# Attention and feed-forward on one core: eight chunks of three tiles in place of nine chunks of two and three

## The chip, the core and the metric

The kernel runs on one core of one Trainium2 chip. The metric is the device time of an execution in microseconds (us). Engines in the text: PE is TensorE, ACT is ScalarE, DVE is VectorE, POOL is GpSimd, SP is SyncE, which here issues nearly all DMAs.

## The reference

Attention over 4 sequences with 8 heads, 768 positions and head size 64. Each position sees a window of the last 128 positions and the first 4 positions (the sinks). The heads' outputs are put side by side (3072 tokens of 512) and go through a feed-forward with d_ff = 2048 and an ELU between two products.

```python
scores = scale * np.matmul(q, k.transpose(0, 1, 3, 2))
rel = pos[:, None] - pos[None, :]
keep = (pos[None, :] < n_sink) | ((rel >= 0) & (rel < window))
scores = np.where(keep, scores, -1e9); scores -= scores.max(-1, keepdims=True)
a = np.exp(scores); a = a / (a.sum(-1, keepdims=True) + 1e-9)
x = heads_side_by_side(np.matmul(a, v))          # 3072 x 512, fp32
h = x @ w_in                                     # 3072 x 2048
g = np.where(h > 0, h, np.exp(np.minimum(h, 0)) - 1)
return (g @ w_out).astype(np.float32)
```

The weights come as float64, 16 MB in all. Results must have about fp32 accuracy, so nearly every product is made of fp16 halves: a value is split into a high half and a residue, and hi*hi, lo*hi and hi*lo are added up in PSUM.

## The kernel before

**Tiles and chunks.** A tile is 128 tokens; there are 24, six a sequence, and tile g is number t = g % 6 in its sequence. Nine chunks (`CHUNKS`) of two or three tiles are worked off in turn: three of two tiles, then six of three. For a chunk, `attention(c)` makes x (four head pairs of 128 columns, `xs[c, q]`) and `feed_forward(c, f0, f1, start)` runs the products over 16 slices f of d_ff: a first stage of 12 matmuls into `h` (L845), the ELU on ACT (L854), POOL or DVE (L856) and DVE (L857), the split of g on ACT (L859) and POOL (L866), and a second stage of 3 matmuls of 512 columns a tile into `acc` (L873). The second stage of an f follows two f later (`LAG`).

**Attention.** Each chunk has one step for each tile and head pair: scores on PE into the banks s0 and s1 (L662 and L663 for split fp16 keys, L668 for fp32), mask and maximum on DVE (L683), exponential on ACT (L688), one plus reciprocal (L692, L697). Keys come by DMA into two slots `kqs` (L568), the first two pairs of chunk 0 ahead of all else (L1249). In the first `DUP` chunks scores are plain fp32 products; in later ones ACT and DVE split the keys first (L577 to L579). A tile with t = 0 has one key block of 128 columns, others have two (260 columns with the sinks). Chunk 0 (`c < PLAIN`) goes on in fp32: a diagonal of the reciprocals on POOL (L704), a product with it on PE that turns the probabilities (L710), an eviction on ACT or DVE (L714), the values in fp32 (L727). All other chunks split the probabilities (L742, L743), turn them with a DMA (L761), and visit PE once for all tiles of a head pair (L775), from chunk `PAIRS` = 3 on once for two pairs. L817 and L818 then make x.

**Weights.** 32 pieces (piece 2f for the first stage, 2f+1 for the second) come by DMA (L354, 512 KB each, at most five ahead of the piece that has been split), and each is rebuilt and split by ACT (L347), DVE (L348), ACT (L507) and POOL (L508, twice).

**Parts.** `PARTS` lets the first two chunks take turns: f 0 to 6 of chunk 0, 0 to 12 of chunk 1, then the rest of chunk 0 and of chunk 1. A chunk's first part stores its sums in `out` through the buffers `sv`; after its second part these are loaded again and added (L912 on).

**Order.** All of this is a list of tasks with rough costs. `Plan.order` puts PE's tasks at wanted positions, works due times backward, runs a list schedule forward, and then applies the changes of `SHIFTS` (each a seed of a random shift of due times or of a line of PE's tasks) one upon the other. Engines then issue in that order; SP issues a load when its task comes up. `with_idle_products` fills planned holes of PE in the first 100 us with products on a constant (L446). Reductions that check the range of inputs (`seen`, `check_v`, `check_kq`) are DVE tasks in the later chunks.

Of the kernel before, what the change touches and what calls it, by code (L numbers as in the profile page):

```python
# [10 lines left out]
F32 = mybir.dt.float32  # L11
# [10 lines left out]
P = 128  # L22
# [20 lines left out]

CHUNKS = [[0, 6], [12, 18], [1, 7], [13, 14, 15], [16, 17, 19], [20, 21, 22], [23, 2, 3], [4, 5, 8], [9, 10, 11]]
SIZES = tuple(len(c) for c in CHUNKS)

HALF = NF // 2
PARTS = [(0,0,7),(1,0,13),(0,7,16),(1,13,16)] + [(c, 0, NF) for c in range(2, len(SIZES))]
LAG = 2
ROUNDS = 8  # L50
SHIFTS = [600047, 600054, 600066, 600067, 600150, 600157, 600163, 600185, 600194, 600295, 600400, 600467, 600483, 600849, 601310, 601684, 602239, 602260, 603167, 603862]
VISIT = 2
# [3 lines left out]
KEEP = 1  # L56
DUP = 3
AHEAD = 5
# [8 lines left out]
PE_T, PE_V = 0.25, 0.13  # L67
RINGS = dict(tp=2, tp_=2, kqs=2, kq=3, vs=2, vm=2, vt=7, sk=2, e=3, st=6, pq=3, pt=6, g=2, gh=3, x=8, wv=4, s0=1, s1=1, po=1, h=2, wu=2, sv=2, wps=1, raw=6)

# [333 lines left out]
def fast_path(tc, ctx, first, kq, vx, wt, out, low, spread, copied, numbers, flag):  # L403
# [26 lines left out]
    xb = pool.tile([P, RINGS["x"] * 2 * TOK_MAX], F16, name="x")  # L430
    sv = rows("sv", [P, DM], F32)
    wv = rows("wv", [P, 512], F32)
# [114 lines left out]
    def attention(c):  # L547
# [12 lines left out]
        def split_keys(h):  # L560
# [13 lines left out]
            if (c, h) not in first["kq"]:  # L574
                ld = add("SP", 0.4, lambda: nc.sync.dma_start(raw, kq[:, o : o + kw]), lat=dma_us(P * kw * 4))
                ld.spare = LATE
            th = add("ACT", act_us(kw), lambda: nc.scalar.activation(hi, raw, AF.Copy, scale=Q_SCALE), deps=[ld])  # L577
# [7 lines left out]
        def vraw(g):  # L585

            if g not in raw_of or raw_of[g][3] < c - KEEP:
                fresh = g not in raw_of
                st, users = vs[slot("vs")], []
                ld = None  # L590
                if not fresh or g not in first["vs_"]:
                    ld = add("SP", 0.4, lambda: nc.sync.dma_start(st, vx[:, g * VT : (g + 1) * VT]), lat=dma_us(P * VT * 4))
                    ld.spare = LATE if c >= DUP else 0.0
                ring("vs", [ld] if ld else [], users)
                raw_of[g] = st, ld, users, c
            raw_of[g] = *raw_of[g][:3], c
            return raw_of[g][:3]
# [15 lines left out]
        def sink_rows(b):  # L613

            if b not in sk_of:
                st, sk, users = vs[slot("vs")], sks[slot("sk")], []
                o = SINKS + b * VT
                ld = add("SP", 0.4, lambda: nc.sync.dma_start(st, vx[:, o : o + VT]), lat=dma_us(P * VT * 4))
                ld.spare = LATE if c >= DUP else 0.0
                va = add("ACT", act_us(VT), lambda: nc.scalar.activation(sk, st, AF.Copy, scale=V_SCALE), deps=[ld])  # L620
                vb = add("DVE", 0.13 + 0.00108 * VT, lambda: nc.vector.scalar_tensor_tensor(sk[64:96, :], st[64:96, :], V_SCALE, sk[64:96, :], ALU.mult, ALU.subtract), deps=[va])
                ring("vs", [ld], [va, vb])
                ring("sk", [va], users)
                sk_of[b] = sk, vb, users
# [200 lines left out]
    def feed_forward(c, f0, f1, start):  # L825
# [77 lines left out]
        for i in range(nt):  # L903
            rows_ = out[CHUNKS[c][i] * P : (CHUNKS[c][i] + 1) * P, :]
            if f1 < NF:
                o = sv[slot("sv")]
            else:
                o = wv[slot("wv")]
            ld = None
            if f0 > 0:  # L910
                ld = add("SP", 0.4, lambda o=o, rows_=rows_: nc.sync.dma_start(o, rows_), deps=[saved[c, i]], lat=dma_us(P * DM * 4))
                ev = add("DVE", dve_us(DM), lambda o=o, i=i: nc.vector.scalar_tensor_tensor(o, acc[i], 1.0 / (G_SCALE * W_SCALE), o, ALU.mult, ALU.add), deps=[s2[i], ld])  # L912
            elif i % 2 or f1 < NF:
                ev = add("ACT", act_us(DM), lambda o=o, i=i: nc.scalar.activation(o, acc[i], AF.Copy, scale=1.0 / (G_SCALE * W_SCALE)), deps=[s2[i]])
            else:
                ev = add("DVE", dve_us(DM), lambda o=o, i=i: nc.vector.tensor_scalar(o, acc[i], 1.0 / (G_SCALE * W_SCALE), None, ALU.mult), deps=[s2[i]])
            sto = add("SP", 0.4, lambda o=o, rows_=rows_: nc.sync.dma_start(rows_, o), deps=[ev], lat=dma_us(P * DM * 4))
            ring("sv" if f1 < NF else "wv", [ld or ev], [sto])
            saved[c, i] = sto
            evacs[i] = ev  # L920

    saved, exps_done, last_g = {}, [], [None]
    start = 0
# [6 lines left out]

    seen = [add("DVE", 0.5, lambda k=k: nc.vector.tensor_reduce(w_top[:, k : k + 1], w[k][:, 0, :], AX.X, ALU.max, apply_absolute_value=True), deps=[w_done[k][0], exps_done[NF * 4 + 2 * k]]) for k in range(NW)]
    def check_v(c, after):
# [26 lines left out]
    for c in range(len(SIZES)):  # L959
        check_v(c, exps_done[NF * 4 + 3 * c])  # L960
    for i in range((len(SIZES) - DUP) * NP):
        check_kq(DUP + i // NP, i % NP, len(SIZES) * NP + i, exps_done[NF * 6 - 4 + 2 * i])

# [33 lines left out]

HINTS = dict(PE=8, ACT=127, DVE=120, SP=61)
E = mybir.EngineType
# [285 lines left out]
```

## Time and profile before

| | us |
|---|---|
| median of 3 runs | 611.33 (611.16 to 611.52) |
| the profiled execution | 611.1 |
| its span, first to last instruction | 609.3 |
| PE busy | 601.2 |
| DVE, ACT, POOL busy | 481.8, 428.1, 308.3 |
| DMA: moved, share of the span | 105.21 MB, 67.4% on SP's queue |

A busy PE is not a PE at useful work: the products on a constant count as busy. Timelines list a run of like instructions as one row with start, length and count; the start of the next row tells when PE went on, since matmuls overlap at their ends.

### The profile page before, as it was taken

How to read it: one execution, taken by the hardware profiler on the slowest of the kernel's cores; microseconds unless marked ns; L12 is line 12 of the kernel's file. 1: busy time of each engine (PE TensorE's matmuls, PEld its weight loads, DVE VectorE, ACT ScalarE, POOL GpSimd, SP SyncE). 2: the span in 40 equal slices, each digit the busy share in tenths (PEclk: the TensorE clock that was granted, in tenths of full speed). 3: DMA queues.
4: the chain of work that ended last, by engine and by line, in shares of the span. 5: the costliest groups of instructions: out<-in, count | busy, mean ns of one | idle time of the engine just before them, and what ended most of it. 6: DMA issues, size and time to landing. Idle time of an engine off the chain costs nothing.

```text
span 609.3 us, 13575 instructions
## 1 busy us (share of the span) xinstructions
PE 601.2 (99%) x4590; PEld 365.7 (60%) x4590; DVE 481.8 (79%) x1211; ACT 428.1 (70%) x1202; POOL 308.3 (51%) x587
## 2 busy tenths in 40 slices
PE   9899999999999999999999999999999999999997
PEld 6666666667765655656565555655656565556664
DVE  6989989799998468899799888799988977543333
ACT  7999999789888567876767766677766756422222
POOL 5876999546555344354544554355554534222221
PEclk9999999999999999999999999999999999999999
DMA  8999987689787346696678955599784883524201
GB/s 311 330 233 267 318 262 227 152 221 209 147 183 188 79 100 118 164 269 126 173 161 247 228 144 133 132 251 221 149 182 105 225 161 75 111 73 113 62 1 56
DMA packets 125998, 105.21 MB, mean 173 GB/s; under 512 B 100580, under 2 KB 100836, under 8 KB 125924
## 3 DMA queue, kind: packets, MB, share of 16 engines
q1 hardware_dynamic: 125780, 104.17, 67.4%
q8 instruction: 37, 0.61, 0.4%
q14 instruction: 37, 0.30, 0.2%
q10 hardware_dynamic: 144, 0.13, 0.1%
HBM read 72.82 MB, written 7.34 MB: 132 GB/s over the span
## 4 chain that ended last, share of the span: by engine, by line
PE 94%; DVE 2%; ACT 2%; issue 1%; POOL 0%; POOLq 0%; DVEq 0%
PE h L845 41%; PE acc L873 40%; PE po L775 3%; PE s L662 3%; PE s L663 3%; PE s L775 2%; PE s L668 1%; PE po L873 1%; PE acc L446 1%; ACT e L688 1%; ACT wu L347 0%; DVE e L683 0%; DVE wv L348 0%; ACT w L507 0%; PE s L780 0%
## 5 line engine op out<-in xcount | busy, mean ns | idle before, releaser
L845 PE MATMUL h<-x,w 128*128 128x384 f16 (+1 forms) x1728 | 273.6, 308 | 0.2
L845 PEld LDWEIGHTS <-w 128*128 128x128 f16 x1728 | 168.4, 98 | 84.4 <-issue 0.7
L866 POOL TENSOR_TENSOR gl<-g,gh 128x384 f16<-128x384 f32 (+1 forms) x144 | 129.3, 898 | 140.7 <-ACT gh L859 132.3
L873 PE MATMUL acc<-w,gh 128*128 128x512 f16 (+1 forms) x768 | 190.3, 375 | 0.0
L873 PEld LDWEIGHTS <-gh 128*128 128x128 f16 x800 | 76.9, 98 | 65.4 <-ACT g L854 1.0
L854 ACT ACTIVATE g<-h 128x384 f32<-128x384 f32 (+1 forms) x144 | 65.0, 451 | 66.8 <-PE h L845 64.9
L743 DVE SCALAR_TENSOR_TENSOR pq<-e,st,pq 128x256 f16<-128x256 f32 (+1 forms) x176 | 100.1, 589 | 14.5 <-ACT pq L742 13.7
L688 ACT ACTIVATE e<-e,st 128x260 f32<-128x260 f32 (+1 forms) x192 | 93.3, 487 | 24.1 <-DVE st L683 23.1
L873 PE MATMUL acc<-w,gl 128*128 128x512 f16 (+1 forms) x384 | 107.8, 375 | 0.0
L859 ACT ACTIVATE gh<-g 128x384 f16<-128x384 f32 (+1 forms) x144 | 69.6, 484 | 54.1 <-DVE g L857 53.4
L683 DVE CUSTOM_DVE_ANT_0 e<-s,m 128x260 f32<-128x260 f32 (+1 forms) x192 | 75.5, 399 | 20.8 <-PE s L663 18.0
L742 ACT ACTIVATE pq<-e,st 128x256 f16<-128x256 f32 (+1 forms) x176 | 79.7, 490 | 13.2 <-DVE st L697 11.9
L857 DVE SCALAR_TENSOR_TENSOR g<-g,h 128x384 f32<-128x384 f32 (+1 forms) x144 | 72.4, 503 | 12.3 <-POOL g L856 11.1
L856 POOL TENSOR_SCALAR g<-g 128x384 f32<-128x384 f32 (+1 forms) x77 | 42.0, 545 | 63.5 <-ACT g L854 62.7
L856 DVE TENSOR_SCALAR g<-g 128x384 f32<-128x384 f32 (+1 forms) x67 | 27.9, 417 | 50.2 <-ACT g L854 49.5
L873 PEld LDWEIGHTS <-gl 128*128 128x128 f16 x400 | 39.1, 98 | 44.2 <-POOL gl L866 0.7
L577 ACT ACTIVATE kq<-kqs 128x912 f16<-128x912 f32 (+1 forms) x48 | 48.5, 1010 | 8.7 <-PE s L663 6.1
L508 POOL TENSOR_TENSOR w<-wv,w 128x256 f16<-128x256 f32 x64 | 53.0, 846 | 2.8 <-ACT w L507 2.1
L692 POOL TENSOR_SCALAR st<-st 128x2 f32<-128x2 f32 x83 | 25.0, 301 | 47.0 <-ACT e L688 41.9
L578 DVE SCALAR_TENSOR_TENSOR kq<-kqs,kq 128x528 f16<-128x528 f32 (+1 forms) x48 | 39.3, 820 | 2.6 <-ACT kq L577 2.1
L662 PE MATMUL s<-kq 128*128 128x260 f16 x144 | 39.5, 275 | 0.0
L663 PE MATMUL s<-kq 128*128 128x260 f16 x144 | 39.5, 274 | 0.0
(105 smaller groups left out, 671.1 us busy)
## 6 DMA issues: line engine op xcount, KB each, us to landing
raw<-in_wt_dram SPq DMA_DIRECT2D x32, 512.0 KB, 5.8
kqs<-in_kq_dram SPq DMA_DIRECT2D x24, 522.0 KB, 3.9
kqs<-in_kq_dram SPq DMA_DIRECT2D x24, 456.0 KB, 4.2
vs<-in_vx_dram SPq DMA_DIRECT2D x34, 256.0 KB, 3.5
vm<-in_kq_dram SPq DMA_DIRECT2D x24, 261.0 KB, 4.2
out_dram<-wv SPq DMA_DIRECT2D x23, 256.0 KB, 2.4
vm<-in_kq_dram SPq DMA_DIRECT2D x24, 228.0 KB, 4.3
vm<-in_vx_dram SPq DMA_DIRECT2D x9, 512.0 KB, 5.3
```

The source lines that it names most:

```text
L662: nc.tensor.matmul(sp[:, :wd], q, hi[:, c0 : c0 + wd], start=True, stop=False)
L683: red = add("DVE", 0.08 + 0.00103 * wd, lambda ee=ee, me=me, sp=sps[e], m=m, wd=wd, to_score=to_score: nc.vector.tensor_tensor_reduce(ee, ...
L688: ex = add("ACT", 0.278 + 0.00083 * wd, lambda ee=ee, me=me, rs=rs[:, e : e + 1]: nc.scalar.activation(ee, ee, AF.Exp, bias=me, scale=-1.0 ...
L742: a = add("ACT", act_us(nb * P, True), lambda src=src, hi=hi, re=re: nc.scalar.activation(hi, src, AF.Copy, scale=re), deps=[rr])
L743: b = add("DVE", 0.45 if nb == 2 else 0.3, lambda src=src, hi=hi, lo=lo, re=re: nc.vector.scalar_tensor_tensor(lo, src, re, hi, ALU.mult, ...
L845: nc.tensor.matmul(hp[:, :n], win[:, part, d, :], xx[:, :n], start=k == 0, stop=k == 3 * ND - 1)
L854: a = add("ACT", 0.13 + 0.00091 * n, lambda gf=gf, hp=hp, sums=sums: nc.scalar.activation(gf, hp[:, :n], AF.Exp, scale=1.0 / G_SCALE, accu ...
L856: b = add("DVE", 0.06 + 0.00057 * n, lambda gf=gf: nc.vector.tensor_scalar(gf, gf, -1.0, G_SCALE, ALU.add, ALU.mult), deps=[a], slow=2.1, ...
L857: b = last_g[0] = add("DVE", dve_us(n), lambda gf=gf, hp=hp: nc.vector.scalar_tensor_tensor(gf, gf, 0.0, hp[:, :n], ALU.min, ALU.max), dep ...
L859: th = add("ACT", act_us(n), lambda gf=gf, gh=gh: nc.scalar.activation(gh[:, :n], gf, AF.Copy), deps=[b])
L866: tls.append(add("POOL", pool_us(cut), lambda gl=gl, gf=gf, gh=gh, cut=cut: nc.gpsimd.tensor_tensor(gl[:, :cut], gf[:, :cut], gh[:, :cut], ...
L873: nc.tensor.matmul(bank[:, cs], gg[:, i * P : (i + 1) * P], wout[:, part, cs], start=f == f0 and k == 0, stop=f == f1 - 1 and k == 2)
```

## The change

The tiles are grouped anew: eight chunks of three. `PARTS` runs each chunk in one piece, and what stored, loaded and added partial sums goes, with the buffers `sv`; the room gives `vs` a third slot. `DUP` falls to 2, so the first two chunks (six tiles, as before) have fp32 scores. `PLAIN` stays 1, so chunk 0 with its fp32 path has three tiles. `LATE`, a margin on loads in the plan, applies from chunk 3 as before. The range checks hang on other exponentials of the same kind. `SHIFTS` is another list, of 36 seeds in place of 20 (left out below), and `HINTS`, which places a branch hint in each engine's queue, has new counts.

```diff
--- before.py
+++ after.py
@@ -41,20 +41,19 @@
 V_MAX, EXP_MAX, W_MAX, W_MIN = 31.0, 2900.0, 65000.0, 0.25
 
 
-CHUNKS = [[0, 6], [12, 18], [1, 7], [13, 14, 15], [16, 17, 19], [20, 21, 22], [23, 2, 3], [4, 5, 8], [9, 10, 11]]
+CHUNKS = [[0, 6, 12], [18, 19, 20], [21, 22, 23], [13, 14, 15], [16, 17, 1], [2, 3, 4], [5, 7, 8], [9, 10, 11]]
 SIZES = tuple(len(c) for c in CHUNKS)
 
-HALF = NF // 2
-PARTS = [(0,0,7),(1,0,13),(0,7,16),(1,13,16)] + [(c, 0, NF) for c in range(2, len(SIZES))]
+PARTS = [(c, 0, NF) for c in range(len(SIZES))]
 LAG = 2
 ROUNDS = 8
...
 VISIT = 2
 PAIRS = 3
 LATE = 1.0
 SPARE = 0.1
 KEEP = 1
-DUP = 3
+DUP = 2
 AHEAD = 5
 HELD = 3
 HALVES = (slice(0, DM // 2), slice(DM // 2, DM))
@@ -65,7 +64,7 @@
 V_AT0 = 5.0
 T_AT = 3.5
 PE_T, PE_V = 0.25, 0.13
-RINGS = dict(tp=2, tp_=2, kqs=2, kq=3, vs=2, vm=2, vt=7, sk=2, e=3, st=6, pq=3, pt=6, g=2, gh=3, x=8, wv=4, s0=1, s1=1, po=1, h=2, wu=2, sv=2, wps=1, raw=6)
+RINGS = dict(tp=2, tp_=2, kqs=2, kq=3, vs=3, vm=2, vt=7, sk=2, e=3, st=6, pq=3, pt=6, g=2, gh=3, x=8, wv=4, s0=1, s1=1, po=1, h=2, wu=2, wps=1, raw=6)
 
 
 def key_tiles(ch):
@@ -428,7 +427,6 @@
     ghs = rows("gh", [P, TOK_MAX], F16)
     gls = rows("gl", [P, TOK_MAX], F16, RINGS["gh"])
     xb = pool.tile([P, RINGS["x"] * 2 * TOK_MAX], F16, name="x")
-    sv = rows("sv", [P, DM], F32)
     wv = rows("wv", [P, 512], F32)
     wu = rows("wu", [P, 512], I32)
     rawb = pool.tile([P, RINGS["raw"], 1025], I32, name="raw")
@@ -573,7 +571,7 @@
             ld = None
             if (c, h) not in first["kq"]:
                 ld = add("SP", 0.4, lambda: nc.sync.dma_start(raw, kq[:, o : o + kw]), lat=dma_us(P * kw * 4))
-                ld.spare = LATE
+                ld.spare = LATE if c >= 3 else 0.0
             th = add("ACT", act_us(kw), lambda: nc.scalar.activation(hi, raw, AF.Copy, scale=Q_SCALE), deps=[ld])
             tk = add("DVE", 0.155 + 0.00106 * kc, lambda: nc.vector.scalar_tensor_tensor(lo, raw[:, :kc], Q_SCALE, hi[:, :kc], ALU.mult, ALU.subtract), deps=[th], slow=1.5)
             tq = add("DVE", 0.18 + 0.00106 * qc, lambda: nc.vector.scalar_tensor_tensor(hi[D:, kc:], raw[D:, kc:], Q_SCALE, hi[D:, kc:], ALU.mult, ALU.subtract), deps=[th], slow=1.5)
@@ -590,7 +588,7 @@
                 ld = None
                 if not fresh or g not in first["vs_"]:
                     ld = add("SP", 0.4, lambda: nc.sync.dma_start(st, vx[:, g * VT : (g + 1) * VT]), lat=dma_us(P * VT * 4))
-                    ld.spare = LATE if c >= DUP else 0.0
+                    ld.spare = LATE if c >= 3 else 0.0
                 ring("vs", [ld] if ld else [], users)
                 raw_of[g] = st, ld, users, c
             raw_of[g] = *raw_of[g][:3], c
@@ -616,7 +614,7 @@
                 st, sk, users = vs[slot("vs")], sks[slot("sk")], []
                 o = SINKS + b * VT
                 ld = add("SP", 0.4, lambda: nc.sync.dma_start(st, vx[:, o : o + VT]), lat=dma_us(P * VT * 4))
-                ld.spare = LATE if c >= DUP else 0.0
+                ld.spare = LATE if c >= 3 else 0.0
                 va = add("ACT", act_us(VT), lambda: nc.scalar.activation(sk, st, AF.Copy, scale=V_SCALE), deps=[ld])
                 vb = add("DVE", 0.13 + 0.00108 * VT, lambda: nc.vector.scalar_tensor_tensor(sk[64:96, :], st[64:96, :], V_SCALE, sk[64:96, :], ALU.mult, ALU.subtract), deps=[va])
                 ring("vs", [ld], [va, vb])
@@ -902,24 +900,16 @@
             nt -= 1
         for i in range(nt):
             rows_ = out[CHUNKS[c][i] * P : (CHUNKS[c][i] + 1) * P, :]
-            if f1 < NF:
-                o = sv[slot("sv")]
-            else:
-                o = wv[slot("wv")]
-            ld = None
-            if f0 > 0:
-                ld = add("SP", 0.4, lambda o=o, rows_=rows_: nc.sync.dma_start(o, rows_), deps=[saved[c, i]], lat=dma_us(P * DM * 4))
-                ev = add("DVE", dve_us(DM), lambda o=o, i=i: nc.vector.scalar_tensor_tensor(o, acc[i], 1.0 / (G_SCALE * W_SCALE), o, ALU.mult, ALU.add), deps=[s2[i], ld])
-            elif i % 2 or f1 < NF:
+            o = wv[slot("wv")]
+            if i % 2:
                 ev = add("ACT", act_us(DM), lambda o=o, i=i: nc.scalar.activation(o, acc[i], AF.Copy, scale=1.0 / (G_SCALE * W_SCALE)), deps=[s2[i]])
             else:
                 ev = add("DVE", dve_us(DM), lambda o=o, i=i: nc.vector.tensor_scalar(o, acc[i], 1.0 / (G_SCALE * W_SCALE), None, ALU.mult), deps=[s2[i]])
             sto = add("SP", 0.4, lambda o=o, rows_=rows_: nc.sync.dma_start(rows_, o), deps=[ev], lat=dma_us(P * DM * 4))
-            ring("sv" if f1 < NF else "wv", [ld or ev], [sto])
-            saved[c, i] = sto
+            ring("wv", [ev], [sto])
             evacs[i] = ev
 
-    saved, exps_done, last_g = {}, [], [None]
+    exps_done, last_g = [], [None]
     start = 0
     for c, f0, f1 in PARTS:
         if f0 == 0:
@@ -928,7 +918,7 @@
         start += 2 * (f1 - f0)
 
 
-    seen = [add("DVE", 0.5, lambda k=k: nc.vector.tensor_reduce(w_top[:, k : k + 1], w[k][:, 0, :], AX.X, ALU.max, apply_absolute_value=True), deps=[w_done[k][0], exps_done[NF * 4 + 2 * k]]) for k in range(NW)]
+    seen = [add("DVE", 0.5, lambda k=k: nc.vector.tensor_reduce(w_top[:, k : k + 1], w[k][:, 0, :], AX.X, ALU.max, apply_absolute_value=True), deps=[w_done[k][0], exps_done[NF * 3 + 2 * k]]) for k in range(NW)]
     def check_v(c, after):
         t, n = vm[slot("vm")].rearrange("p a w -> p (a w)"), SIZES[c] * P
         src = vx[:, (ENDS[c] - SIZES[c]) * VT : ENDS[c] * VT].rearrange("p (g w) -> p g w", g=SIZES[c])
@@ -957,9 +947,9 @@
         seen.extend(new)
 
     for c in range(len(SIZES)):
-        check_v(c, exps_done[NF * 4 + 3 * c])
+        check_v(c, exps_done[NF * 3 + 3 * c])
     for i in range((len(SIZES) - DUP) * NP):
-        check_kq(DUP + i // NP, i % NP, len(SIZES) * NP + i, exps_done[NF * 6 - 4 + 2 * i])
+        check_kq(DUP + i // NP, i % NP, len(SIZES) * NP + i, exps_done[len(exps_done) - 6 - 2 * ((len(SIZES) - DUP) * NP - i)])
 
     def before():
         for r, most in ((es_of[:, 1:], EXP_MAX), (v_top, V_MAX)):
@@ -995,7 +985,7 @@
 VERBOSE = False
 
 
-HINTS = dict(PE=8, ACT=127, DVE=120, SP=61)
+HINTS = dict(PE=8, ACT=94, DVE=120, SP=45)
 E = mybir.EngineType
 QUEUES = dict(PE=E.PE, ACT=E.Activation, DVE=E.DVE, SP=E.SP)
```

## Rows read from the trace of the kernel before

**Rows 1.** The page: the span, and each engine's busy time, share and instructions.

```profile
span 609.3 us, 13575 instructions
...
PE 601.2 (99%) x4590; PEld 365.7 (60%) x4590; DVE 481.8 (79%) x1211; ACT 428.1 (70%) x1202; POOL 308.3 (51%) x587
```

**Rows 2.** Windows: length, busy us of PE, PEld, DVE, ACT, POOL; clock, DMA.

```profile
10.00:20.00 10.00, 8.75 (x68) 6.07 (x67) 8.76 (x27) 9.82 (x31) 8.81 (x13) 1.00 0.96 354
20.00:30.00 10.00, 9.00 (x78) 6.43 (x78) 8.48 (x35) 9.41 (x33) 7.97 (x12) 1.00 0.94 347
27.72:61.90 34.18, 33.63 (x273) 21.71 (x270) 30.83 (x97) 34.18 (x117) 24.87 (x44) 1.00 0.96 260
62.00:110.00 48.00, 48.00 (x381) 31.46 (x382) 44.55 (x88) 46.92 (x131) 45.64 (x57) 1.00 0.81 258
178.00:250.00 72.00, 72.00 (x543) 41.63 (x542) 52.42 (x133) 51.31 (x136) 30.58 (x61) 1.00 0.54 121
400.00:500.00 100.00, 100.00 (x778) 58.09 (x777) 90.03 (x204) 69.88 (x188) 50.78 (x107) 1.00 0.83 182
```

**Rows 3.** PE's timeline, the start: start, us, line, operation, count.

```profile
4.27 0.49 PE L668 MATMUL s<-kqs 64*128 64x128 f32 x4
...
8.33 0.49 PE L668 MATMUL s<-kqs 64*128 64x128 f32 x4
...
9.40 0.44 PE L727 MATMUL po<-pt,vs 128*64 128x128 f32 x4
...
13.89 0.49 PE L668 MATMUL s<-kqs 64*128 64x128 f32 x4
...
19.13 0.70 PE L668 MATMUL s<-kqs 64*128 64x128 f32 x4 [0.58 <-DVE st L683]
...
27.72 1.47 PE L845 MATMUL h<-x,w 128*128 128x256 f16 x12
```

**Rows 4.** SP's timeline: the load of the third head pair's keys.

```profile
6.31 0.33 SPq L568 DMA_DIRECT2D kqs<-in_kq_dram  x1
```

**Rows 5.** The view of tile kqs, 6 to 8 us: that load's landing.

```profile
DMA to landing us min/median/max: 6.8/6.8/6.8
```

**Rows 6.** Windows, PE alone: the DMA's GB/s is the last column.

```profile
8.00:10.00 2.00, 2.00 (x18) 1.00 1.02 416
12.00:14.00 2.00, 1.83 (x17) 1.00 1.04 408
```

**Rows 7.** PE's timeline: first stages of successive f, two tiles, then three.

```profile
72.52 1.47 PE L845 MATMUL h<-x,w 128*128 128x256 f16 x12
...
75.12 1.47 PE L845 MATMUL h<-x,w 128*128 128x256 f16 x12
...
538.35 2.11 PE L845 MATMUL h<-x,w 128*128 128x384 f16 x12
...
542.24 2.11 PE L845 MATMUL h<-x,w 128*128 128x384 f16 x12
```

**Rows 8.** PE's timeline: two visits, an f with a wide score.

```profile
38.54 0.25 PE L775 MATMUL po<-pt,vh 128*64 128x128 f16 x2
...
39.00 1.48 PE L845 MATMUL h<-x,w 128*128 128x256 f16 x12
...
60.45 1.47 PE L845 MATMUL h<-x,w 128*128 128x256 f16 x12
...
63.80 1.47 PE L845 MATMUL h<-x,w 128*128 128x256 f16 x12
...
67.81 0.30 PE L775 MATMUL po<-pt,vh 128*64 128x128 f16 x4
...
68.61 1.04 PE L873 MATMUL acc<-w,gh 128*128 128x512 f16 x4
```

**Rows 9.** Groups of POOL by shape: count, busy us, mean ns, idle before.

```profile
L866 POOL TENSOR_TENSOR gl<-g,gh 128x384 f16<-128x384 f32 x95 | 90.4, 952 | 126.0 <-ACT gh L859 121.0 <-issue 4.2
...
L508 POOL TENSOR_TENSOR w<-wv,w 128x256 f16<-128x256 f32 x64 | 53.0, 846 | 2.8 <-ACT w L507 2.1
```

More of the change, by code (lines that the diff above doesn't have):

```diff
@@ L41 @@
 V_MAX, EXP_MAX, W_MAX, W_MIN = 31.0, 2900.0, 65000.0, 0.25
-CHUNKS = [[0, 6], [12, 18], [1, 7], [13, 14, 15], [16, 17, 19], [20, 21, 22], [23, 2, 3], [4, 5, 8], [9, 10, 11]]
+CHUNKS = [[0, 6, 12], [18, 19, 20], [21, 22, 23], [13, 14, 15], [16, 17, 1], [2, 3, 4], [5, 7, 8], [9, 10, 11]]
 SIZES = tuple(len(c) for c in CHUNKS)
-HALF = NF // 2
-PARTS = [(0,0,7),(1,0,13),(0,7,16),(1,13,16)] + [(c, 0, NF) for c in range(2, len(SIZES))]
+PARTS = [(c, 0, NF) for c in range(len(SIZES))]
 LAG = 2
 ROUNDS = 8
-SHIFTS = [600047, 600054, 600066, 600067, 600150, 600157, 600163, 600185, 600194, 600295, 600400, 600467, 600483, 600849, 601310, 601684, 602239, 602260, 603167, 603862]
+SHIFTS = [7000020, 7000061, 7000067, 7000128, 7000202, 7000237, 7000246, 7000268, 7000272, 7000307, 7000441, 7000520, 7000523, 7000539, 7000579, 7000614, 7000907, 7001079, 7001093, 7001174, 7001179, 7001758, 7001996, 7002607, 7002617, 7002623, 7002624, 7002735, 7002873, 7003005, 7003193, 7004872, 7005450, 7009092, 7012293, 7016138]
 VISIT = 2
```

## The prediction

> **What bounds the kernel now.** I read the page first: TensorE (PE) counts as busy for 601.2 of 609.3 us [rows 1], so only what PE has to do, and the places where it can't do it, can move the time. The table by stages comes second [rows 2]: from 62 us on PE is busy for the whole of every stretch, while ACT, DVE and POOL have room (in 178 to 250, ACT 51.3 and POOL 30.6 of 72 us; DVE comes near its limit only in 400 to 500, 90.0 of 100, and PE still never waits). Before that it is the other way round: from 10 to 62 us ACT is busy nearly without a break (34.18 of 34.18 in 27.72 to 61.90), DVE and POOL follow, and 62 to 110 has POOL at 45.64 of 48. That is where the 32 weight pieces are split, beside the attention of the first chunks. The third view, PE's timeline of the first 28 us [rows 3], shows what the busy share hides: between the scores and values stand filler products on a constant (L446), which are no work. The first product of the feed-forward is at 27.72.
>
> So the end is: the start T of the feed-forward, plus the work PE still has to do then, plus the holes after T. I forecast each.
>
> **The work after T.** The feed-forward is the same 24 tiles in other groups. One f (a slice of 128 of d_ff) takes 2.60 us with two tiles and 3.89 with three [rows 7]. 48 f of two tiles become 32 of three: 48 x 2.60 = 124.8 becomes 32 x 3.89 = 124.5, so -0.3. The wider matmul gains nothing here. Splitting the first two chunks in parts, and its removal, changes no matmul either: what goes are four stores, four loads and adds of partial sums, on SP and on ACT and DVE after 27 us; PE reads none of it, so they count as nothing, hidden by PE's own work; without that cover they are four evictions of about half a us.
>
> The set of tiles with fp32 scores keeps its size (0, 6, 12, 18, 1, 7 become 0, 6, 12, 18, 19, 20: four first tiles of a sequence, two others), so the scores cost the same in both. What differs is tile 12: it moves from chunk 1 into chunk 0, the plain one, where probabilities are turned on PE and values are fp32. Its four scores move ahead of T (0.49 us by the row, 0.42 up to the next start [rows 3], so -1.7 after T). Its fp16 values vanish. Two visits show their price: 38.54 to 39.00 for two tiles of one key block, 67.81 to 68.61 for two tiles of two blocks [rows 8], so 0.34/2 = 0.17 a block and 0.12 a visit. That is 4 x 0.17 = 0.7 less, and with 18 visits in place of 20 another 0.2. The sum of work after T: -0.3 - 1.7 - 0.7 - 0.2 = **-2.9 us**. The checks keep their number and their distance from the end of the kernel; they run on DVE, where PE never waited for them.
>
> Break-even is therefore at T = 27.72 + 2.9 = 30.6, if the holes after T stay the same.
>
> **The start T.** Chunk 0 now has 12 steps (three tiles, four head pairs) in place of 8, and its plain path is on the way to T. Before, four steps came at once, one each (8.33 - 4.27)/3 = 1.35 us; then came a wait until 13.89 for the keys of the third head pair; then four more at (19.13 - 13.89)/3 = 1.75; and 8.6 us after the last score the feed-forward began [rows 3]. The wait is a DMA: issued at 6.31, landed 6.8 later, at 13.1 [rows 4, 5], behind the first loads and four weight pieces. The third tile fills this wait with two steps that are free: six steps from about 4.7 last until 12.8.
>
> But the same keys come later. The buffer they go to has two slots, freed by the scores of pair 0, which are now three, so the issue comes after a fifth weight piece (the first five wait for nothing). Ahead of them stood 2 x 260 KB of keys, 2 x 256 KB of values and 4 x 512 KB of weights; now 2 x 390, 3 x 256 and 5 x 512 KB. With their own 390 for 260 KB that is 1158 KB, or 1.19 MB, more; at 408 to 416 GB/s [rows 6] 2.9 us, so they land at about 16.0. The Trainium skill ("DMA: Bandwidth & Descriptors", section "Where 436 GB/s comes from") puts what HBM gives one core at some 358 GB/s. By that figure the delay would be an estimated 3.3 us and the forecast 0.4 us later; this trace disagrees, with more than 400 over several windows, and the sum goes by the trace.
>
> From 16.0 six steps are left. At 1.35 the last score is at 22.8, at 1.75 at 24.8. From the last score to T it takes 8.6 as before, or, where nothing else is in the way, what the first step shows: 5.1 from score to values, 0.4 for those and about 0.8 for the two evictions, 6.4. So T lies between 29.2 and 33.4. I take the pace of 1.35 and 7.5 us, the middle of the two tails: during the wait until 16.0 ACT and DVE can do the five pieces that have landed, which in the old order stood between the later steps; the tail stays mixed, since ACT goes on with pieces. **T = 30.3, +2.6.**
>
> **The holes after T.** Between the first feed-forward product (27.72) and 61.86 I count on PE's timeline eleven first stages (the first at 27.72, the last at 60.45 [rows 3, 8]), eight second-stage groups of 1.30, five scores of 0.42 and four of 0.64, and four visits: 31.0 us of work in 34.1, so 3.1 of holes and fillers. There each new f brings two weight pieces, and two tiles use them in 2.6 us. With three tiles PE needs a new f every 3.89, and with chunk 1's own attention (3.35 in place of 2.60 where a wide score lies in an f [rows 8], and one visit a head pair, 10.7 us in all) every 4.6. Against that POOL has 4 x 0.846 for the two pieces, 0.952 for the residue of g [rows 9] and some 0.3 of chunk 1's, 4.7 together: level with PE, and covered by the pieces done before T, of which four are enough. ACT has less to do per us of PE than before. I take 1.6 of holes, -1.5; the bounds are 0 and 5.
>
> **Sum.** +2.6 - 2.9 - 1.5 = -1.8 us. The profiled execution took 611.1 with a span of 609.3; 611.1 - 1.8 = 609.3, and the median of the runs lies 0.2 higher: **609.5 us**. Chunk 2 now has split fp16 scores, so its key splits come one chunk sooner; six chunks have them in both kernels, and ACT has 21 of 72 us free in a stretch of such work [rows 2], so nothing for that. The end (last outputs, last chunk of tiles 9 to 11) is as before.
>
> **The rivals.** A run here can tell 0.2% from no change, 1.2 us: below 610.1 is faster, above 612.6 slower.
> - *The chain of chunk 0 stays slow (slower).* If the six late steps keep 1.75 us and the tail 8.6, T = 33.4, and with holes as before the time is 611.3 + 5.7 - 2.9 = 614.1. It decides from T = 31.8 on (1.2 past break-even). For it: DVE at 8.76 and ACT at 9.82 of 10 us from 10 to 20 [rows 2]. Against: part of that load is done earlier. 0.15.
> - *POOL becomes the bound of the first chunk (slower).* If its residues run slower beside DVE (1.2 in place of 0.95) and few pieces are done by T, it needs 4.9 to PE's 4.6 and loses up to 5 us over 16 f: T as forecast, 611.3 - 0.3 + 1.9 = 612.9. For it: POOL at 95% in 62 to 110 [rows 2], where PE still didn't wait. 0.08.
> - *A wash (same).* T at 30.6 to 32, holes as much as before or a little less: 610.2 to 612.5. All terms here are small and cancel. 0.25.
> - *A bigger gain.* T at the low bound, 29.2, and no holes: 611.3 + 1.5 - 2.9 - 3.1 = 606.8; with an order that starts chunk 0's last pair earlier, 605.5. This belongs to faster. 0.15.
>
> **How the numbers follow.** The forecast, 606.8 to 610.1 about 609.5, has 0.37; with the bigger gain, faster has 0.52. The wash is 0.25, the two slower ones 0.23. Most of the chance is on two signs: the likeliest case's own range is 607 to 611. Leaving out a tenth at each end, the range goes from 605.5 to 614.0.
>
> **What would show it.** In PE's timeline after: the seventh fp32 score at about 16 (not 14 or 18), the first feed-forward matmul at 29 to 32, fewer filler products between 30 and 60, an f of 3.89 from the first chunk on, and a visit of three tiles for each pair of chunks 1 and 2. From 62 us on PE should be full in every stretch. The prediction is wrong if the first f comes after 32 or before 28, if PE waits for weights (L508, L507) in the first chunk, or if a hole opens at a chunk's border, where nothing here predicts one.

## The result and the profile after

The changed kernel takes 615.13 us (median of 4 runs, 613.81 to 616.17) against 611.34 (611.16 to 611.52, 4 runs) of the kernel before: the ratio is 1.006 [1.0045, 1.0075], so it is slower by 0.6%. Two later comparisons agree: 1.0061 [1.0035, 1.0087] and 1.0042 [1.0027, 1.0056]. The prediction, 609.5 and faster, is wrong.

The profiled execution took 613.81 us with a span of 612.0, 2.7 more than the 611.1 and 609.3 of before. It is the fastest of the four runs, so the profiles account for 2.7 of the 3.8 us between the medians; the rest is in runs that left no trace. The table by stages of after answers to [rows 2]:

```profile
span 612.0 us, 13002 instructions
...
10.00:20.00 10.00, 8.54 (x71) 6.32 (x72) 8.49 (x27) 9.52 (x31) 7.89 (x11) 1.00 0.88 329
20.00:30.00 10.00, 9.04 (x72) 6.12 (x69) 8.59 (x36) 9.81 (x36) 8.49 (x14) 1.00 0.69 246
27.72:61.90 34.18, 32.77 (x228) 18.59 (x228) 31.83 (x79) 32.99 (x93) 28.57 (x42) 1.00 0.97 291
62.00:110.00 48.00, 48.00 (x345) 25.84 (x344) 44.22 (x98) 46.35 (x126) 44.17 (x60) 1.00 0.82 207
178.00:250.00 72.00, 72.00 (x543) 41.55 (x541) 54.43 (x138) 53.53 (x145) 30.56 (x56) 1.00 0.66 140
400.00:500.00 100.00, 100.00 (x771) 57.91 (x769) 84.61 (x199) 70.42 (x189) 49.49 (x102) 1.00 0.75 173
```

From 62 us on PE is full, as before. So the difference lies ahead of that, and PE's timeline shows it, the answer to [rows 3]:

```profile
4.75 0.49 PE L666 MATMUL s<-kqs 64*128 64x128 f32 x4 [0.50 <-DMA kqs<-in_kq_dram]
...
11.36 0.49 PE L666 MATMUL s<-kqs 64*128 64x128 f32 x4
...
16.95 0.49 PE L666 MATMUL s<-kqs 64*128 64x128 f32 x4
17.38 1.22 PE L444 MATMUL acc<-const-bfloat16-1.0 128*128 128x240 bf16 x10
18.78 0.70 PE L666 MATMUL s<-kqs 64*128 64x128 f32 x4 [0.18 <-DVE st L681]
...
26.99 0.49 PE L666 MATMUL s<-kqs 64*128 64x128 f32 x4
...
34.65 4.06 PE L843 MATMUL h<-x,w 128*128 128x384 f16 x24
...
40.29 2.11 PE L843 MATMUL h<-x,w 128*128 128x384 f16 x12 [1.16 <-DVE g L855]
```

The six early scores of chunk 0 start from 4.75 to 11.36, the six late ones from 16.95 to 26.99, and the feed-forward starts at T = 34.65, 6.93 later than before. The one hole after T that the trace names is the 1.16 us ahead of 40.29.

To see what PE did, I took each row of the whole timeline from its start to the start of the next (or to the idle time ahead of that) and added by kind, in both kernels:

| PE, us | before | after | difference |
|---|---|---|---|
| feed-forward, both stages | 501.94 | 501.08 | -0.86 |
| fp16 scores and values | 66.53 | 65.56 | -0.97 |
| fp32 scores | 13.17 | 12.83 | -0.34 |
| turning of probabilities (L710, after L708) | 4.71 | 7.58 | +2.87 |
| fp32 values (L727, after L725) | 3.14 | 4.37 | +1.23 |
| fillers, idle, start-up sums | 15.53 | 16.22 | +0.69 |
| end of the last product | 605.02 | 607.64 | +2.62 |

Work is +1.93 of the 2.62, waiting +0.69. (In the profiles of the two repeats below, c1 and d2, the same count gives +2.1 of work in both, and +0.8 and +1.1 of waiting.) The work that grew is all tile 12's plain path: 48 products of each kind now, 32 before.

```profile
L708 PE MATMUL acc<-pq,e 128*128 128x128 f32 x48 | 8.5, 300 | 0.7 <-POOL pq L702 0.6
...
L725 PE MATMUL po<-pt,vs 128*64 128x128 f32 x48 | 5.0, 296 | 1.4 <-ACT pt L712 0.5 <-DVE x L816 0.4 <-DVE pt L712 0.4
```

What follows T became shorter, from 577.30 to 572.99 us: -4.31, where the forecast had -2.9 of work and -1.5 of holes, -4.4. So the sum of the forecast's second half was met, though its two terms were not, and T, 34.65 in place of 30.3, makes the miss.

### The profile page after: what moved, and what is told of

It is laid out like the page before. It is cut to its first block, busy times and chain, and to the rows that moved or that the text cites. A ratio compares the mean times of both kernels' runs of the same rounds, so it can differ in the third digit from the quotient of the medians.

```text
span 612.0 us, 13002 instructions
## 1 busy us (share of the span) xinstructions
PE 602.6 (98%) x4406; PEld 349.0 (57%) x4406; DVE 469.6 (77%) x1166; ACT 422.6 (69%) x1152; POOL 300.6 (49%) x554
## 4 chain that ended last, share of the span: by engine, by line
PE 93%; ACT 3%; DVE 2%; DMA 1%; issue 1%; POOL 0%; SPq 0%; POOLq 0%
PE h L843 40%; PE acc L871 40%; PE po L773 3%; PE s L660 3%; PE s L661 3%; PE s L773 2%; ACT e L686 1%; PE s L666 1%; PE po L871 1%; ACT wu L346 1%; DMA kqs<-in_kq_dram 1%; DVE wv L347 1%; PE po L778 0%; ACT w L505 0%; DVE e L681 0%
## 5 line engine op out<-in xcount | busy, mean ns | idle before, releaser
L843 PE MATMUL h<-x,w 128*128 128x384 f16 x1536 | 270.3, 326 | 1.2 <-DVE g L855 1.2
L843 PEld LDWEIGHTS <-w 128*128 128x128 f16 x1536 | 149.8, 98 | 98.2 <-issue 1.8
L864 POOL TENSOR_TENSOR gl<-g,gh 128x384 f16<-128x384 f32 x128 | 124.6, 973 | 156.6 <-ACT gh L857 149.5
L871 PE MATMUL acc<-w,gh 128*128 128x512 f16 (+1 forms) x768 | 187.5, 375 | 0.0
L741 DVE SCALAR_TENSOR_TENSOR pq<-e,st,pq 128x256 f16<-128x256 f32 (+1 forms) x168 | 97.5, 600 | 16.4 <-ACT pq L740 15.6
L852 ACT ACTIVATE g<-h 128x384 f32<-128x384 f32 x128 | 62.1, 486 | 69.2 <-PE h L843 65.8
L686 ACT ACTIVATE e<-e,st 128x260 f32<-128x260 f32 (+1 forms) x192 | 93.0, 485 | 22.1 <-DVE st L681 20.3
L857 ACT ACTIVATE gh<-g 128x384 f16<-128x384 f32 x128 | 66.5, 520 | 55.8 <-DVE g L855 54.9
L855 DVE SCALAR_TENSOR_TENSOR g<-g,h 128x384 f32<-128x384 f32 x128 | 70.2, 548 | 14.3 <-POOL g L854 12.9
L854 POOL TENSOR_SCALAR g<-g 128x384 f32<-128x384 f32 x70 | 41.3, 590 | 70.0 <-ACT g L852 69.4
L854 DVE TENSOR_SCALAR g<-g 128x384 f32<-128x384 f32 x58 | 23.9, 412 | 51.0 <-ACT g L852 50.7
L506 POOL TENSOR_TENSOR w<-wv,w 128x256 f16<-128x256 f32 x64 | 51.0, 819 | 2.6 <-ACT w L505 2.1
L686 ACT ACTIVATION_READ_ACCUMULATOR e<-e,st 128x1 f32 x192 | 36.2, 189 | 0.0
```

The costliest lines, as they stand in the source:

```text
L686: ex = add("ACT", 0.278 + 0.00083 * wd, lambda ee=ee, me=me, rs=rs[:, e : e + 1]: nc.scalar.activation(ee, ee, AF.Exp, bias=me, scale=-1.0 ...
L741: b = add("DVE", 0.45 if nb == 2 else 0.3, lambda src=src, hi=hi, lo=lo, re=re: nc.vector.scalar_tensor_tensor(lo, src, re, hi, ALU.mult, ...
L843: nc.tensor.matmul(hp[:, :n], win[:, part, d, :], xx[:, :n], start=k == 0, stop=k == 3 * ND - 1)
L852: a = add("ACT", 0.13 + 0.00091 * n, lambda gf=gf, hp=hp, sums=sums: nc.scalar.activation(gf, hp[:, :n], AF.Exp, scale=1.0 / G_SCALE, accu ...
L854: b = add("DVE", 0.06 + 0.00057 * n, lambda gf=gf: nc.vector.tensor_scalar(gf, gf, -1.0, G_SCALE, ALU.add, ALU.mult), deps=[a], slow=2.1, ...
L855: b = last_g[0] = add("DVE", dve_us(n), lambda gf=gf, hp=hp: nc.vector.scalar_tensor_tensor(gf, gf, 0.0, hp[:, :n], ALU.min, ALU.max), dep ...
```

## The experiments

Two theories were to be told apart. The first: T sets the end, and T is late through the keys of the third head pair, which have to queue behind weight pieces, and through the slow steps behind them; then what moves T moves the end. The second: the splitting of 32 weight pieces on ACT, DVE and POOL, beside the attention there, sets how soon the first 110 us can be over; then an earlier T is given back in holes. (In the later expectations Theory K is the first and Theory W the second.) A third suspicion was the search of the order. Each kernel ran beside the kernel before (medians 611.21, 612.02 and 611.82 in the three sets). Where the edit changes the plan, the exchanges of the order were searched anew, except in the two kernels that have none. In c2, c3, c4, e1 and e3 a second edit is in force: fillers stand only ahead of the first feed-forward product. In c4, d3, e1, e2 and e3 PE's first products are slow until 8 to 10 us (last section), so their first late scores come 1.3 to 2.3 us later and their T is only roughly comparable.

**c1_again** and **d2_again**: the changed kernel again, no edit.

> The changed kernel once more, for its spread: its four runs so far lie between 613.81 and 616.17 us, those of before between 611.16 and 611.52. Both theories below expect 613.8 to 616.2 again. If the first feed-forward product (T) is at 34.65 us in this profile too, the spread of the runs has another place than the start; if the keys of the third head pair land at another time than 16.6 us and T moves with them, the DMAs of the start make the spread.

> The changed kernel as it is, beside d1_fill on the same chip: 614 to 617.3 with a median of 615.1 to 615.7, under both theories. If its profile is one of the longer executions, Theory A expects first scores of 0.8 us in place of 0.49 in it, and Theory B 0.49 throughout with the loss elsewhere.

615.59 (614.04 to 617.26) and 614.69 us (613.84 to 616.16), with T at 34.74 and 35.18. The loss and the late T repeat. So the spread of the runs has another place than T, as far as these profiles show; d2's median lies a little below the range that was expected.

**c3_slot3**: the keys' buffer gets a third slot, so the third load no longer waits.

```
-RINGS = dict(tp=2, tp_=2, kqs=2, kq=3, ...
+RINGS = dict(tp=2, tp_=2, kqs=3, kq=3, ...
```

> The changed kernel with three slots for keys in place of two, so that the third pair's keys are issued with the first loads and wait for no score; shifts searched anew. Theory 1: they land by 9 to 11 us, the steps of chunk 0 follow each other from 4.7 on without the wait until 16.95, T is 30 to 32, the time 610.5 to 612.5. Theory 2: T stays at 33.5 or later, since ACT and DVE do the same weight pieces in the same time; 613 to 616.

615.56 us, ratio 1.0069 [1.0042, 1.0096]: no gain over the changed kernel. SP's and PE's timelines:

```profile
3.70 0.43 SPq L566 DMA_DIRECT2D kqs<-in_kq_dram  x1
...
4.77 0.49 PE L666 MATMUL s<-kqs 64*128 64x128 f32 x4 [0.69 <-DMA kqs<-in_kq_dram]
...
21.56 0.54 PE L666 MATMUL s<-kqs 64*128 64x128 f32 x4
...
30.33 4.07 PE L843 MATMUL h<-x,w 128*128 128x384 f16 x24
...
80.03 0.27 PE L660 MATMUL s<-kq 128*128 128x260 f16 x1 [1.71 <-DVE st L681]
...
81.01 0.27 PE L660 MATMUL s<-kq 128*128 128x260 f16 x1 [0.59 <-DVE st L681]
...
81.23 3.31 PE L843 MATMUL h<-x,w 128*128 128x384 f16 x12
```

The keys are issued at 3.70 and T comes at 30.33, 4.3 earlier. That this is the forecast's 30.3 is chance: there is no wait here, the twelve scores follow at (21.56 - 4.77)/11 = 1.53 us, and 8.77 us pass from the last one to T. But PE's last product ends at 607.56 (607.64 without the edit). After T there are 2.55 us more of idle time, and the products take 1.7 longer: the first stage at 81.23 takes 3.31 us, where it takes 2.11 at 40.29 above. The holes are waits for the softmax of a later chunk, at a time when the windows show ACT, DVE and POOL full:

```profile
78.00:80.00 2.00, 0.33 (x4) 0.10 (x1) 1.94 (x5) 2.00 (x8) 1.81 (x2) 1.00 1.04 311
80.00:82.00 2.00, 1.37 (x9) 0.87 (x9) 1.83 (x4) 2.00 (x7) 2.00 (x4) 0.99 1.08 394
82.00:84.00 2.00, 2.00 (x8) 0.91 (x6) 2.00 (x4) 1.78 (x6) 1.79 (x3) 0.50 1.05 422
```

The last weight residue on POOL (the second half of the last piece) starts at 111.3 us; in the changed kernel, with T 4.3 later, at 110.4. The view of the line in both, the changed kernel first (duration in ns, first and last start):

```profile
L506 POOL TENSOR_TENSOR w<-wv,w x64: 662/720/1209, 13.7 to 110.4; 128x256 f16<-128x256 f32 x64
...
L506 POOL TENSOR_TENSOR w<-wv,w x64: 663/790/1215, 14.3 to 111.3; 128x256 f16<-128x256 f32 x64
```

So the wait for the keys does cost T some 4 us, and an earlier T is given back within the first 110 us. Neither expectation was met whole: T is the first theory's, the time the second's. A part of the gain shows in the spans: their median is 612.2 us over c3's six runs, and 612.8 to 613.8 over the runs of the changed kernel in its three sets. In time it is lost, for 3.3 to 3.6 us lie outside the span in every run of c3 and 1.8 in the changed kernel's.

**d4_before_slot3**: the same third slot in the kernel before.

```
-RINGS = dict(tp=2, tp_=2, kqs=2, kq=3, ...
+RINGS = dict(tp=2, tp_=2, kqs=3, kq=3, ...
```

> The kernel before with a third slot for keys (shifts searched anew), so that the third pair's keys wait for no score. If T counts by itself: T falls from 27.7 to 24 to 25.5 and the time to 608 to 610. Theory W: an earlier T is given back as holes between 30 and 110 us, where the weights come no sooner (last residue of a weight at 108.5 before): 610.5 to 612.5.

614.26 us, ratio 1.0034 [1.0015, 1.0053], slower. T is 25.16, 2.6 earlier, and the last product ends at 605.76 instead of 605.02: 4.9 us of fillers and holes after T, 1.2 before. Two of the holes:

```profile
30.01 1.47 PE L845 MATMUL h<-x,w 128*128 128x256 f16 x12 [0.81 <-DVE g L857]
...
42.99 0.71 PE L668 MATMUL s<-kqs 64*128 64x260 f32 x4 [0.86 <-DVE st L683]
```

The last residue starts at 112.2 (108.5 in the kernel before).

```profile
L508 POOL TENSOR_TENSOR w<-wv,w x64: 663/718/1191, 11.9 to 108.5; 128x256 f16<-128x256 f32 x64
```

An earlier T is given back once more; the time is 1.8 us above the upper end of what theory W expected.

**c4_late4**: the split of pieces 4 to 31 waits for chunk 0's last x, so that ACT and DVE are free for chunk 0.

```
+                if c == 0 and q == NP - 1:
+                    for piece in range(4, NW):
+                        w_ld[piece][1].deps.append(fa)
```

> The changed kernel, where the splits of weight pieces 4 to 31 wait in the plan until chunk 0's last x is made; two slots for keys as before; shifts searched anew. Theory 1: the keys land at 16 to 17 as in the changed kernel and the wait before them stays, so T falls by 1 us at most. Theory 2: the steps after the keys follow at 1.35 us in place of 2.0, T falls by 3 to 4 us to about 31, and the time is lost again after T as holes in the first chunk, where weights come late: 614 to 618 in all.

622.95 us, ratio 1.0165 [1.0133, 1.0198]. The late steps run at (25.49 - 18.22)/5 = 1.45 us, in the changed kernel at (26.99 - 16.95)/5 = 2.0, and T is 32.10 although the first late score comes 1.3 later.

```profile
18.22 0.49 PE L667 MATMUL s<-kqs 64*128 64x128 f32 x4
...
25.49 0.49 PE L667 MATMUL s<-kqs 64*128 64x128 f32 x4
```

What ACT does between those scores in the changed kernel, its split steps alone, L346 and L505:

```profile
17.47 0.63 ACT L505 ACTIVATE w<-wv 128x512 f16<-128x512 f32 x1 [0.43 <-DVE wv L347]
18.01 0.77 ACT L346 ACTIVATE wu<-raw 128x512 f16<-128x512 bf16 x1
18.64 0.61 ACT L505 ACTIVATE w<-wv 128x512 f16<-128x512 f32 x1
...
19.92 0.62 ACT L505 ACTIVATE w<-wv 128x512 f16<-128x512 f32 x1
...
21.49 0.76 ACT L346 ACTIVATE wu<-raw 128x512 f16<-128x512 bf16 x1
...
23.61 0.77 ACT L346 ACTIVATE wu<-raw 128x512 f16<-128x512 bf16 x1
...
25.00 0.77 ACT L346 ACTIVATE wu<-raw 128x512 f16<-128x512 bf16 x1
...
26.01 0.78 ACT L346 ACTIVATE wu<-raw 128x512 f16<-128x512 bf16 x1 [0.19 <-DVE pt L712]
```

Eight split steps, 5.7 us of ACT in ten. In c4 there are two (18.28 and 19.10) between the late scores. So the pace is that of ACT and DVE shared with the split (e1 below shows the same). What is put off there is paid for later and dearer: 8.4 us idle after T, among them these, and the last residue at 115.0. The pace is theory 2's; the time is 5 us beyond it, of which 2.2 lie outside the span (4.0 us there, 1.8 in the changed kernel).

```profile
67.42 0.83 PE L667 MATMUL s<-kqs 64*128 64x128 f32 x4 [1.64 <-DVE st L682]
...
85.55 1.96 PE L847 MATMUL h<-x,w 128*128 128x384 f16 x11 [1.69 <-POOL w L506]
```

**c2_hold**: weight pieces 2 to 4 are loaded only after the last score of head pair 0, so that the keys pass them.

```
+                if c == 0 and k == nt - 1:
+                    for piece in (2, 3, 4):
+                        w_ld[piece][0].deps.append(scs[-1])
```

> The changed kernel, with the loads of weight pieces 2 to 4 placed behind the last score of head pair 0 of chunk 0, so that they are issued behind the keys of the third head pair; the list of shifts is searched anew. Theory 1 (T is late because these keys stand behind five weight pieces): 1536 KB or 1.57 MB less ahead of them at 0.41 MB/us is 3.8 us, the keys land at about 12.8 in place of 16.6, T falls from 34.65 to 31 to 32, and the time to 611 to 612.5. Theory 2 (the pace of the late steps is set by the weight splits that share ACT and DVE, whenever the keys come): the keys land early, but T stays at 33.5 or later and the time within 1 us of the changed kernel.

617.24 us, ratio 1.0076 [1.0049, 1.0104]. The profiled execution is the slowest, 619.34, and PE's products run longer in its first 20 us (last section), so the keys were issued at 9.3 instead of 7.44 and T is 37.44. It fits neither theory and doesn't tell what it was made for.

**d1_fill**: three more fillers ahead of the first score, where PE idles 0.50 us.

```
-    extra, free, done = {}, 0.0, []
+    extra, free, done = {0: [Task("PE", IDLE_US, product, (), [], 0.0, None, 1.0) for _ in range(3)]}, 0.0, []
```

> The changed kernel with three more products on a constant, between the product that spreads the scalars and the first score, where its PE idles for 0.50 us because the longer first keys land at 4.7 us (before: no idle there). Theory A (what the runs of the changed kernel have over its profile, a median of 615.1 to 615.6 against profiles of 613.8 and 614.1, is PE working at half pace for part of the first 20 us in most executions, as the profile of c2_hold shows it with scores of 0.80 us up to 20.3, and the hole ahead of the first score favours it): the spread shrinks and the median falls to 613.8 to 614.3. Theory B (the spread comes from elsewhere, or the pace does not hang on this hole): the median stays at 615 to 615.7, with runs up to 617.

614.98 us (613.79 to 616.46) beside 614.69 (613.84 to 616.16) without: neither the time nor the spread of the runs changes, so theory A isn't borne out; the median lies just below what theory B expected.

**d3_unsplit**: the kernel before, its first two chunks run in one part each.

```
-PARTS = [(0,0,7),(1,0,13),(0,7,16),(1,13,16)] + [(c, 0, NF) for c in range(2, len(SIZES))]
+PARTS = [(c, 0, NF) for c in range(len(SIZES))]
```

> The kernel before with its nine chunks, where no chunk is run in two parts (that part of the change alone; shifts searched anew). Theory W (the first 110 us are bound by the weight work on ACT, DVE and POOL, and the parts were there because two tiles use up a pair of pieces in 2.6 us): chunk 0 alone needs its 16 f in 42 us, the weights come at 4.7 us a pair, so PE idles some 10 us and more in the first 110 us: 619 to 625. Rival (the parts only keep PE busy where the attention would do as well): within 2 us of before, 611 to 613.5.

623.07 us, ratio 1.0166 [1.0128, 1.0203]. T is 29.45, but after it 11.9 us go to fillers and holes, 1.2 before. PE over 30 to 90 us:

```profile
30.00:90.00 60.00, 54.03 (x427) 35.51 (x426) 51.95 (x128) 55.73 (x170) 49.08 (x65) 0.97 0.92 259
```

With two tiles a chunk, one f needs its two pieces every 2.6 us and the split can't follow, though it is done sooner than in any other run with the whole split:

```profile
L508 POOL TENSOR_TENSOR w<-wv,w x64: 661/714/1127, 13.9 to 94.4; 128x256 f16<-128x256 f32 x64
```

Here the last residue starts at 94.4 us, so the 108 to 112 us of the kernels above are no limit of the split by itself: more likely they come from the way the split and the attention of the first chunks share ACT, DVE and POOL, which no run shows by itself. The parts let chunk 1's f use pieces that chunk 0 has had. Three tiles do the same by using each piece longer: holes after T stay at 1.2 without parts. On that point the change does what the forecast said.

**e1_light_after** and **e2_light_before**: both kernels without DVE's step of the split, so with weights of fewer bits and with 32 DVE steps of some 1 us fewer.

```
-            b = add("DVE", 0.72, steps[1], deps=[a], slow=1.5)
-            ring("wu", [a], [b])
-            ring("raw", [ld], [a, b])
+            b = a
+            v = top.bitcast(F32)
+            ring("raw", [ld], [a])
```

> The changed kernel without the DVE step of each weight piece (L347, 32 times 0.7 to 1.2 us): the low bits of the weights are left out, so the product is computed with weights of fewer bits; shifts searched anew. Theory W (the first 110 us are bound by the weight work that shares DVE, ACT and POOL with the attention, and T and the holes only share out one loss): T falls by 2 us or more, the holes after T don't grow, and the time falls by 2 to 5 us, to 610 to 613. Theory K (T is set by the landing of the third pair's keys at 16.6 and the chain behind it): T stays within 1 us of 34.7 and the time within 1 us of the changed kernel.

> The kernel before with the same step left out, shifts searched anew. Theory W: it gains as well, 1.5 to 4 us, and the distance between the two kernels (2.5 us between their profiles) shrinks to the 1.9 us of PE work that tile 12 brings to chunk 0, less what three tiles fill better: 0 to 2 us. Theory K: before gains as much as or more than the changed kernel, so the distance stays at 2.5 or grows.

613.55 us, ratio 1.0026 [1.0012, 1.0041], and 610.71, ratio 0.9978 [0.9961, 0.9994]. In e1 DVE is busy for 73.3 of the first 110 us (96.4 with the step), the late steps take (25.94 - 18.51)/5 = 1.49, T is 33.07, the last residue starts at 100.7, and no hole is left after T:

```profile
span 608.7 us, 12900 instructions
...
18.51 0.49 PE L666 MATMUL s<-kqs 64*128 64x128 f32 x4
...
25.94 0.49 PE L666 MATMUL s<-kqs 64*128 64x128 f32 x4
...
0.00:110.00 110.00, 106.80 (x744) 61.93 (x745) 73.33 (x246) 102.71 (x293) 84.98 (x156) 1.00 0.85 262
```

Of the two profiles, the span falls by 3.3 us in the changed kernel and not at all in the one before (609.3), but both have the slow first products of the last section. The spans of all runs are better evidence: their median is 608.8 us over e1's ten runs and 608.9 over e2's, beside 612.8 to 613.8 for the changed kernel and 609.4 to 610.2 for the one before. By spans, then, leaving out the step gains the changed kernel 4 to 5 us and the other about 1, and the distance between them is gone, as theory W expected. By time the changed kernel gains only 1 to 2 us and the distance stays, 2.84, as theory K expected: in each of e1's runs 4.1 to 5.2 us lie outside the span, in each of e2's 1.8 or 1.9. T speaks against K as well. So what the engines do supports W, the whole time doesn't, and why e1 has more time outside its span is open.

**e3_unsearched_after** and **e4_unsearched_before**: no exchanges in the order.

```
-SHIFTS = [7000020, 7000061, ...]
+SHIFTS = []
```

> The changed kernel with an empty list of shifts, so with the schedule as it is before the search. If the search is worth anything on the chip, this is 1 to 4 us slower than the changed kernel, with a later T or more holes before 110 us; if the search only fits the plan's own costs, within 1 us.

> The kernel before with an empty list of shifts. If the new search were the cause of the loss (a better search of the old kernel against a poorer one of the new), before loses 2 us or more without its search, to 613 to 616. If not, it stays within 1 us of 611 to 612.5.

618.44 us, ratio 1.0097 [1.0047, 1.0147], and 612.11, ratio 1.0002 [0.9979, 1.0024]. The search is worth some 2 to 3 us in the changed kernel (1.0097 beside 1.0042 to 1.0061) and nothing measurable in the one before. It reduces the loss and isn't its cause.

## Why the prediction was wrong

**What bounds it: half right.** That PE's work, T and the holes make the end is an identity, and it served to book the time. Read as a cause it failed: c3 and d4 brought T forward by 4.3 and 2.6 us and the last product came 0.1 earlier and 0.7 later. [rows 2] had ACT at 34.18 of 34.18 and POOL at 45.64 of 48; the forecast named them and still priced T as if each us of it were a us of the end.

**Work and holes after T: the sum met by luck.** -2.9 of work and -1.5 of holes were forecast. By the kinds after T: feed-forward -0.86, fp32 scores 7.61 to 5.17, which is -2.44, and fp16 scores and values -0.97, together -4.3 with holes of 1.16 in place of 1.19 (fillers and idle). So the sum of -4.4 was met by two misses that cancel: work fell by 1.4 more than forecast, and the -1.5 of holes didn't come, because there were hardly any to gain. Of the 3.1 that the forecast had counted between 27.72 and 61.86 as holes and fillers (2.9, for its terms add up to 31.2 of work and not 31.0), the rows of the kernel before name 1.2, and the rest lies in the distances between products, which the table above books as work.

**T: the step that failed.** Forecast 16.0 + 5 x 1.35 + 7.5 = 30.3; measured 16.95 + 5 x 2.0 + 7.66 = 34.65, beyond the 32 that the prediction named as its sign of being wrong. Three terms:
- The late score at 16.95, +0.95. The third keys' load is issued at 7.44, behind a fifth weight piece as forecast, and takes 9.2 us, to 16.64.

```profile
3.71 2.97 SPq L353 DMA_DIRECT2D raw<-in_wt_dram  x5
7.44 0.33 SPq L566 DMA_DIRECT2D kqs<-in_kq_dram  x1
```

  The windows of 2 us from 8 to 16 show 411, 422, 408 and 404 GB/s, so the rate was as forecast; two of them, PE alone:

```profile
10.00:12.00 2.00, 1.85 (x16) 1.00 1.03 422
...
14.00:16.00 2.00, 1.80 (x19) 1.00 1.03 404
```

  The Trainium skill ("DMA: Bandwidth & Descriptors", section "Where 436 GB/s comes from") would have given an estimated 16.4 by its 358 GB/s, nearer to 16.64; the windows, above 400, don't bear that cause out, and what made the 0.6 us is not shown.
- The pace of the late steps, 2.0 in place of 1.35: 5 x 0.65, +3.3, three quarters of the miss. The forecast had ACT and DVE do the five landed pieces during the wait. In the trace only two of the five were through ACT's last step (L505 at 12.47 and 15.12) by 16.95, no more than the kernel before had at its first late score, 3.1 us sooner (L507 at 10.97 and 13.28), for ACT and DVE had the two extra steps of chunk 0 to do there as well; the rest stood between the late steps. c4 and e1, with less split work there, show 1.45 and 1.49. The upper bound of 1.75, from the kernel before, was exceeded too.
- The tail, 7.66 for 7.5.

**"Two steps that are free": wrong.** They stood where PE waited, but the wait moved with them: from the start of the last early score to that of the first late one it is 5.56 us before (8.33 to 13.89) and 5.59 after (11.36 to 16.95). And they took ACT and DVE from the split. A sum over PE would have warned: with T at 30.3, PE has to do the tile's turning, values and scores before T, 6.2 us more by the table's kinds (2.87, 1.23, and 2.10 of scores), in 2.6 us more of time. So the waiting before T would have had to fall by 3.6; it rose by 0.7. The tile's turning and fp32 values also cost PE 4.1 us wherever they stand, against 0.97 saved in fp16; the forecast moved work across T and never wrote that net of the whole down.

**The rivals.** The chain that stays slow, T = 33.4 and 614.1, was nearest, and the slow pace was its mechanism. Its time, 614.1, is close, yet c3 shows that a faster chain would not have won it back. POOL as a bound of the first chunk was not seen: in the changed kernel PE did not wait for L506 after T (in c3 it did once, for 0.43 us). Search, parts and the later chunks: as forecast, no loss (62 us and on; d3, e4).

What the runs don't settle is how the 2.6 us divide: +1.9 is PE's work, but the kernel before also has 15.5 us of waiting, and whether supply or work is the limit of the changed kernel is only bounded by e1, where the span fell by 3.3 with less split work. Nor do they settle how much of what c3 and d4 lost after T belongs to their orders: each was searched by itself, e3 shows that a search can be worth 2 to 3 us, and c3 had no fillers after T, where its clock fell (last section). By time no variant was faster than the kernel before but e2, which splits weights of fewer bits.

## What to carry to other kernels

When a first block is made larger to fill a hole of the busiest engine, price the block on the engines that feed it: a hole filled there is free only if those engines are idle in it as well. Before a start is priced as part of the end, find what else the stage after it waits for (here ACT, DVE and POOL, which share the weights' split with the attention until about 110 us): in c3 and d4 an earlier start was given back there. And add the busiest engine's work over the whole kernel as a check on any sum that only moves it past a point.

## What was not expected of the hardware

In some profiles PE's first products take longer although the windows print a granted clock of 1.00. In c2_hold they do so until 20.3 us with hardly a gap:

```profile
4.00:20.00 16.00, 15.70 (x75) 1.00 0.87 310
...
18.08 0.80 PE L667 MATMUL s<-kqs 64*128 64x128 f32 x4
...
20.96 0.49 PE L667 MATMUL s<-kqs 64*128 64x128 f32 x4
```

The columns of the first line are window, length, PE busy, granted clock, DMA share, GB/s. A score takes 0.80 us that takes 0.49 later, and five fillers 1.18 that take 0.69 in the changed kernel. But the clock record in the trace doesn't cover this time. Its first entry, at full clock, starts at 20.2 us in c2, at 8.6 to 9.9 in c4, d3, e1, e2 and e3, and at 3.5 to 4.8 in all other profiles (3.9 in the changed kernel, 4.1 in the one before); a window prints 1.00 where there is no entry. How long a score takes at the lower clock, d4 shows at a time that is recorded, with 0.50 granted, that is 1.2 of 2.4 GHz:

```profile
18.00:20.00 2.00, 2.00 (x10) 0.50 0.11 40
...
18.91 0.80 PE L668 MATMUL s<-kqs 64*128 64x128 f32 x4
```

So by their lengths c2's first products ran at the lower clock up to 20.2 us, while PE was busy for 15.70 of 16 us. The first fifteen fillers take 3.0 to 3.2 us in all fourteen profiles (ten of the same take 1.22 at 17.38 in the changed kernel), so by that measure each starts low, and the profiles differ in when it ends. What decides that is not shown. In c4, e1 and e3 the first late score comes at 18.22, 18.51 and 18.86, 1.3 to 1.9 us later than in the changed kernel. Whether it makes the spread of 3 to 4 us among runs of one kernel was not shown either, and d1 did not change it.

In c3 a wait of PE (0.33 of 2 us busy in 78 to 80) was followed by a granted clock of 0.50, that is 1.2 of 2.4 GHz, in 82 to 84: a hole of 1.7 us was followed by 1.2 more in the next stage.

The time outside the span is 1.8 or 1.9 us in every run of both kernels, but 3.3 to 3.6 in all six runs of c3, 4.0 or 4.1 in those of c4 and 4.1 to 5.2 in those of e1. No run tells why.
